# Softmax's end in two halves, an output sum in two parts, and phi's last steps moved, in a fused attention and FFN kernel on one core

## The chip, the core and the metric

The kernel runs on one core of one Trainium2 chip. Its time is the device time of one execution in microseconds (us). Five engines matter here, each with an instruction queue of its own that is worked off in order: TensorE (PE, with PEld for its weight loads), VectorE (DVE), ScalarE (ACT), SyncE (SP, which here only issues DMAs) and the DMA engines behind SP's queue. An instruction that waits holds up everything behind it in its queue.

## What is computed

```python
def _attn_ref(q, k, v, phi):                 # 8 batches, 8 heads, seq 576, head_dim 64; phi has 32 columns
    a = phi - np.max(phi, axis=2, keepdims=True)      # softmax of phi along the sequence
    a = np.exp(a); a = a / (np.sum(a, axis=2, keepdims=True) + 1e-09)
    k_m = np.einsum('bhsm,bhsd->bhmd', a, k)          # 32 memory rows a head
    v_m = np.einsum('bhsm,bhsd->bhmd', a, v)
    scores = (1/8) * np.matmul(q, k_m.transpose(0, 1, 3, 2))
    scores = scores - np.max(scores, axis=-1, keepdims=True)
    attn = np.exp(scores); attn = attn / (np.sum(attn, axis=-1, keepdims=True) + 1e-09)
    return np.matmul(attn, v_m)

def _moe_ref(x, w_in, w_out):                # x: 4608 x 512, d_ff 2048
    h = x @ w_in
    g = h * (1.0 / (1.0 + np.exp(-h)))
    return g @ w_out
```

## The kernel before

The kernel works through the eight batches one after the other. While the FFN of batch b runs, the attention of batch n = b + 1 is prepared beside it, and phi of batch m = b + 2 is begun. The FFN's first weight is folded with the attention's values (`p_mm`), so the FFN reads the attention's probabilities directly. All large operands are split in a high and a low part (`hi`, `lo`), and each product is made of three matmuls.

For batches 2 to 7 the FFN has 16 **slots**, eight for each half of the sequence (`t`). In slot s

- PE makes `h` (L807, 12 matmuls), then the matmuls of the slot's events, then, by `finish`, the 21 products L846 of the slot before (`st_step`);
- ACT applies Silu to `h` (L821 and L823; `gbuf` is one buffer), and makes high parts (L825, L835);
- DVE forms sums in `gbuf` (L826, L829, L830) and makes low parts (L836, L837). These five DVE instructions are called F(s) below.

The products are summed by a Strassen-like scheme in four PSUM banks (`sums`). After each half, `st_out` copies two banks on ACT (L877), adds on DVE (L882, seven adds) and stores two tiles of 128x512. The four banks are used again by the next half, so its products wait for the last add that reads them. After batches 1, 3, 5 and 7 a **left-over pass** handles the last 64 rows of two batches: `left_split` (L680, L682) splits `gleft` in four pieces, and L846 multiplies them into `lsum`.

The other work is put in slots by a table of events: `ev(b, slot, fn, ...)`. Events of one slot run in the order in which they were put there, after that slot's F(s). For slots (not for the left-over pass) every DVE instruction of an event is tied behind the slot's last split (`behind`); the framework's scheduler then sets the final order in each queue. Around the change these events stand:

- `s_max`, `s_sub`, `s_exp`, `s_sum`, `s_norm` (L424 to L442): the scores' softmax of batch n, slots 9 to 13, on the whole sequence `ALL`.
- `s_back` (slot 14): DVE transposes the probabilities (L454, two of 128x576), ACT writes the high part of the half `FIRST` (L459, in `s_high`), `s_low` the low part (L464). The other half, `SECOND`, gets its parts in slot 1 of the next batch.
- `p_mm` (L628): a fold into PSUM tile `bg`, of which there is one; ACT and DVE read it (L644, L646) before the next `p_mm` may write it. Slots 13 and 15, and slots 1 and 2 of the next batch.
- `phi_max`, `phi_fold`, `phi_sub`, for batch m: the maximum over the sequence. `phi_fold` turns it with a transpose (L284, L286), gathers four rows of 32 partitions side by side by four small copies (L292), reduces (L294), spreads the result by three small copies (L296), and turns it back (L301, L302); `phi_sub` subtracts it (L310, L313). Slots 11 and 15; for batch 2, slots 13 and 15.
- `win_load`: SP loads a quarter of the saved first weight (1 MB) in slots 10, 12 and 14 and in slot 0 of the next batch; each waits until PE is through with that place's last reader.

SP's queue is in order as well: loads, stores and anything else that it issues wait behind one another.

Of the kernel before, what the change touches and what calls it, by code (L numbers as in the profile page):

```python
# [10 lines left out]
F32 = mybir.dt.float32  # L11
# [14 lines left out]
NFC = DFF // P  # L26
CW = 256
JW = 512
NJ = DFF // JW
HALF = S // 2  # L30
MAIN = 512
LEFT = S - MAIN
NI = MAIN // P
# [15 lines left out]
def attn_ffn_kernel(  # L49
# [9 lines left out]
    nc = tc.nc  # L59
    const = ctx.enter_context(tc.tile_pool(name="const", bufs=1))  # L60
    sb = ctx.enter_context(tc.tile_pool(name="sb", bufs=2))
# [216 lines left out]
            for i, p in enumerate(ps_):  # L278
                at[b]["am", p] = pm[:, i * P : (i + 1) * P]

    def phi_fold(b, step):
        if step == 0:
            t = sb.tile([P, HM], F32, tag="am", name="mxt", bufs=1)
            nc.vector.transpose(t, at[b]["mx"].rearrange("p g f -> p (g f)"))  # L284
            qm = sb.tile([P, H], F32, tag="qm", name="qm", bufs=1)
            nc.vector.tensor_reduce(qm, t.rearrange("p (n m) -> p n m", m=M), op=ALU.max, axis=AX.X)  # L286
            at[b]["qm"] = qm
        elif step == 1:
            qm = at[b]["qm"]
            z = sb.tile([M, 4, H], F32, tag="qz", name="qz", bufs=1)  # L290
            for i in range(4):
                nc.vector.tensor_copy(z[:, i], qm[M * i : M * (i + 1)])  # L292
            fm = sb.tile([P, H], F32, tag="fm", name="fm", bufs=1)
            nc.vector.tensor_reduce(fm[:M], z.rearrange("p i n -> p n i"), op=ALU.max, axis=AX.X)  # L294
            for i in range(1, 4):
                nc.vector.tensor_copy(fm[M * i : M * (i + 1)], fm[:M])  # L296
            at[b]["fm"] = fm
        else:
            am = sb.tile([P, HM], F32, tag="am", name="am", bufs=1)
            wide = sb.tile([P, H, M], F32, tag="mx", name="wide", bufs=1)  # L300
            nc.vector.tensor_copy(wide, at[b]["fm"].unsqueeze(2).broadcast_to([P, H, M]))  # L301
            nc.vector.transpose(am, wide.rearrange("p n m -> p (n m)"))  # L302
            for p in range(2):
                at[b]["am", p] = am[:, p * P : (p + 1) * P]
# [139 lines left out]
    def set_parts(b):  # L444
        for k, x in enumerate(("ahi", "alo")):
            at[b][x] = aparts[:, k, b == 1].rearrange("p (g s) -> p g s", g=2)

    def s_back(b, u):
        tag = ("x", "y")[b - 1] if b < 3 else "q1"
        at[b]["aT"] = sb.tile([P, 2, S], F32, tag=tag, name=f"aT{b}", bufs=1)  # L450
        set_parts(b)
        aT, sc = at[b]["aT"], at[b]["sc"]
        for p in range(2):
            nc.vector.transpose(aT[:, p], sc[:, p])  # L454
        s_high(b, u)

    def s_high(b, u):
        c = slice(*u)
        nc.scalar.activation(at[b]["ahi"][:, :, c], at[b]["aT"][:, :, c], AF.Copy)  # L459

    def s_low(b, u):
        aT, ahi, alo = (at[b][k] for k in ("aT", "ahi", "alo"))
        c = slice(*u)
        nc.vector.tensor_tensor(alo[:, :, c], aT[:, :, c], ahi[:, :, c], op=ALU.subtract)  # L464

# [208 lines left out]
    def split(g32, steps=(0, 1), gs=None):  # L674
        if gs is None:
            n = next(turn) % 2
            gs = gparts[:, 0, n], gparts[:, 1, n]
        ghi, glo = gs
        if 0 in steps:
            nc.vector.tensor_copy(ghi, g32)  # L680
# [59 lines left out]
    Q = DMODEL // 2  # L740
# [114 lines left out]
    def st_step(b, t, j, part):  # L855
# [14 lines left out]
        if j == NP - 1:  # L870
            st_out(b, t)

    def st_out(b, t):
        o = sb.tile([P, 2, DMODEL], F32, tag="cva", name="oo", bufs=1)
        x = sb.tile([P, 2, Q], F32, tag="cva1", name="x", bufs=1)
        for i in range(2):
            nc.scalar.activation(o[:, i], sums[i], AF.Copy)  # L877
        (c11, c12), (c21, c22) = ((o[:, i, :Q], o[:, i, Q:]) for i in range(2))
        u2, u3 = x[:, 0], x[:, 1]

        def add(to, a, c, op=ALU.add):
            nc.vector.tensor_tensor(to, a, c, op=op)  # L882

        add(u2, sums[2][:, :Q], c11)
        add(u3, sums[2][:, Q:], u2)
        add(c11, c11, c12)
        add(c12, u2, c22)
        add(c12, c12, c21)
        add(c21, u3, sums[3][:, :Q], ALU.subtract)
        add(c22, u3, c22)  # L890
        for i in range(2):
            r = b * S + (2 * t + 1 - i) * P
            nc.sync.dma_start(out[r : r + P], o[:, i])
# [35 lines left out]
    def ev(b, slot, fn, *a):  # L929
        events.setdefault((b, slot), []).append((fn, a))  # L930

    def steady(b, n):


        early = b > 2
        if not early:
            ev(b, 1, phi_max, n)
            for i in range(3):
                ev(b, 2, phi_fold, n, i)
            ev(b, 3, phi_sub, n)  # L940
# [12 lines left out]
        ev(b, 13, s_norm, n, ALL)  # L953
        ev(b, 14, s_back, n, FIRST)
        ev(b, 14, s_low, n, FIRST)
        for k in range(3):
            ev(b, 10 + 2 * k, win_load, n, k)
        for k in range(2):
            ev(b, 13 + 2 * k, p_mm, n, k * JW, JW)
        m = n + 1  # L960
        if m < B:
            ev(b, ex + 3, load_kv, m, range(2))
            ev(b, ex + 3, load_phi, m)
            ev(b, ex + 5, load_q, m, 0)
            ev(b, 7 if early else 12, phi_max, m)
            for i in range(3):
                ev(b, 11 if early else 13, phi_fold, m, i)
            ev(b, 15, phi_sub, m)

    for b in range(B):  # L970
        n = b + 1
        if b == 0:
            for j in range(2, DFF // CW):
                ev(b, 2 * j - 1.5, p_mm, b, j * CW, CW)
        elif b == 1:
            ev(b, 0, win_save)
            for j in range(1, NJ):
                ev(b, 4 * j - 3, p_mm, b, j * JW, JW)
            for j in range(NP):
                ev(b, 1.5 * j + 2, w_forms, j, 0)  # L980
                ev(b, 1.5 * j + 2.5, w_forms, j, 1)
        else:
            ev(b, 0, win_load, b, 3)
            ev(b, 1, p_mm, b, 2 * JW, JW)
            if b > 2:
                ev(b, 1, s_high, b, SECOND)
                ev(b, 1, s_low, b, SECOND)
            ev(b, 2, p_mm, b, 3 * JW, JW)
            if n < B:
                steady(b, n)  # L990
            continue
# [176 lines left out]
    for b in range(B):  # L1168
# [3 lines left out]
        for s in range(NFC if b > 1 else 0):  # L1172
            t, j = divmod(s, NP)
            h = ffn1s(b, t, j)
            part = forms(b, t, j, h)
            for half_slot in range(2):
                for fn, a in events.pop((b, s + half_slot / 2), []):
                    traced = nc.cur_bb.bb.instructions
                    n = len(traced)
                    fn(*a)  # L1180
                    for i in list(nc.cur_bb.bb.instructions)[n:]:
                        if i.engine == DVE and fn is not s_all:
                            behind(i, last_split[-1])
            finish(range(NI))
            prev = ("st", b, t, j, part)
        for fc in range(NFC if b < 2 else 0):
# [23 lines left out]
        if b % 2:  # L1210
            for n in range(NLS):
                gs = left_split(b, n)
                finish((0, 1, 2, 3))
                prev = ("left", b, n, gs)
    finish((0,))
# [55 lines left out]
```

## Time and profile before

| what | value |
|---|---|
| runs | 709.49, 709.56, 711.04 us; median 709.56 us |
| profiled execution | 710.63 us; span from first to last instruction 708.8 us |
| mean granted TensorE clock | 0.994 |
| busy: PE, PEld, DVE, ACT | 681.1, 599.3, 521.9, 361.1 us |
| slots of batches 2 to 7, left-over passes | from about 200 us to the end |

A profile's line of groups reads: line, engine, operation, output<-inputs, shapes, count, then busy time, mean ns of one, and the idle time of the engine ahead of it with what ended it. In a timeline each row is start, duration, engine and instruction; the bracket is the engine's idle time just before and who ended it. Busy times of matmuls overlap: a matmul of 256 columns stands with 0.28 us, but the next one starts 0.12 us later, so that intervals between starts are what PE's pace is read from.

### The profile page before, as it was taken

To read this page: it belongs to the slowest core of one execution; us is meant where nothing else is said; L and a number is where in the kernel's file an instruction comes from. 1 tells how busy PE (TensorE), PEld (TensorE's weight loads), DVE (VectorE), ACT (ScalarE), POOL (GpSimd) and SP (SyncE) were. 2 spreads that over 40 slices of the span, in tenths; PEclk is the share of its full clock that TensorE was granted. 3 is DMA by queue.
4 is the path that set the end of the run, shared out by engine and by line. 5 is a ranking of instruction groups with operands and counts; after the bars stand their busy time and mean duration, and the time that the engine had idled before them with its cause. 6 is when DMAs were issued, how large, how long until landed. Compare 5 with 4: busy or idle time off the path is not lost.

```text
span 708.8 us, 14734 instructions
## 1 busy us (share of the span) xinstructions
PE 681.1 (96%) x5932; PEld 599.3 (85%) x5932; DVE 521.9 (74%) x1109; ACT 361.1 (51%) x664; POOL 0.7 (0%) x6
## 2 busy tenths in 40 slices
PE   8999999999999998899989999999998999999997
PEld 3578777888789898799978999789988899889996
DVE  4898799788847679748976489856885657775653
ACT  3879674534435454743625446464551635554440
POOL 0000000000000000000000000000000000000000
PEclk9999999999999999999999999999999999999999
DMA  9997965314441442243321433234430304310001
GB/s 344 337 349 253 324 253 214 107 43 157 164 137 60 159 149 104 79 154 123 122 90 49 168 121 123 88 96 143 149 120 31 109 2 137 123 40 1 31 1 45
DMA packets 32947, 93.89 MB, mean 132 GB/s; under 512 B 2928, under 2 KB 13296, under 8 KB 29296
## 3 DMA queue, kind: packets, MB, share of 16 engines
q1 hardware_dynamic: 31936, 90.19, 36.8%
q10 hardware_dynamic: 944, 2.77, 1.0%
q8 instruction: 47, 0.77, 0.4%
q14 instruction: 20, 0.16, 0.1%
HBM read 77.22 MB, written 15.73 MB: 131 GB/s over the span
## 4 chain that ended last, share of the span: by engine, by line
PE 61%; DVE 17%; issue 4%; ACT 4%; DVEq 0%; ACTq 0%
PE sum L846 23%; PE h L807 16%; PE acc L706 7%; PE lsum L846 5%; PE h L665 4%; PE bg L628 2%; DVE oo L882 2%; ACT aparts L835 2%; DVE pm L646 2%; DVE gbuf L826 2%; PE accleft L706 2%; PE bg L333 1%; DVE gbuf L829 1%; DVE gbuf L830 1%; DVE aT L454 1%
## 5 line engine op out<-in xcount | busy, mean ns | idle before, releaser
L807 PE MATMUL h<-aparts,pm 128*128 128x288 f32 x1152 | 169.0, 296 | 2.2 <-ACT gleft L823 2.2
L807 PEld LDWEIGHTS h<-aparts,pm 128*128 128x128 f32 x1152 | 157.1, 188 | 3.4 <-ACT gleft L823 2.5
L821 ACT ACTIVATE gbuf<-h 128x512 f32<-128x512 f32 x96 | 57.3, 597 | 140.7 <-PE h L807 140.4
L826 DVE TENSOR_TENSOR gbuf<-gbuf 128x256 f32<-128x256 f32 x96 | 40.4, 421 | 102.8 <-ACT gbuf L821 102.6
L846 PE MATMUL sum<-kept,aparts 128*128 128x256 f32 x576 | 100.8, 284 | 6.4 <-DVE oo L882 6.4
L846 PE MATMUL sum<-wo_hi,aparts 128*128 128x256 f32 x384 | 104.5, 294 | 0.7 <-ACT oo L877 0.7
L846 PE MATMUL sum<-wo_lo,aparts 128*128 128x256 f32 x384 | 100.0, 282 | 0.0
L835 ACT ACTIVATE aparts<-gbuf 128x512 fp32r<-128x512 f32 x86 | 54.4, 633 | 82.7 <-DVE gbuf L830 82.7
L846 PEld LDWEIGHTS sum<-wo_hi,aparts 128*128 128x128 f32 x384 | 72.7, 189 | 22.5 <-ACT gleft L823 10.9
L846 PEld LDWEIGHTS sum<-kept,aparts 128*128 128x128 f32 x576 | 82.5, 191 | 8.0 <-DVE oo L882 8.0
L706 PE MATMUL acc<-wo_hi,gparts 128*128 128x512 f32 x256 | 86.5, 397 | 0.2
L846 PEld LDWEIGHTS sum<-wo_lo,aparts 128*128 128x128 f32 x384 | 73.1, 190 | 0.0
L846 PE MATMUL sum<-wo_hi,gparts 128*128 128x256 f32 x384 | 72.7, 281 | 0.0
L837 DVE TENSOR_TENSOR gparts<-gbuf,aparts 128x512 fp32r<-128x512 f32 x86 | 59.4, 691 | 18.0 <-ACT aparts L835 18.0
L846 PE MATMUL sum<-kept,gparts 128*128 128x256 f32 x288 | 65.5, 282 | 0.0
L706 PEld LDWEIGHTS acc<-wo_hi,gparts 128*128 128x128 f32 x256 | 47.8, 188 | 14.5 <-DVE t L789 1.7
L846 PEld LDWEIGHTS sum<-wo_hi,gparts 128*128 128x128 f32 x384 | 59.4, 190 | 0.0
L665 PEld LDWEIGHTS h<-aparts,pm 128*128 128x128 f32 x372 | 51.8, 188 | 7.7 <-issue 2.3
L665 PE MATMUL h<-aparts,pm 128*128 128x288 f32 x372 | 56.3, 299 | 1.3 <-DVE aparts L464 1.0
L706 PE MATMUL acc<-wo_lo,gparts 128*128 128x512 f32 x128 | 50.5, 394 | 0.8 <-DVE wo_lo L182 0.7
L825 ACT ACTIVATE aparts<-gbuf 128x384 fp32r<-128x384 f32 x96 | 50.4, 525 | 0.0
L846 PEld LDWEIGHTS sum<-kept,gparts 128*128 128x128 f32 x288 | 47.9, 190 | 0.0
(200 smaller groups left out, 995.2 us busy)
## 6 DMA issues: line engine op xcount, KB each, us to landing
win<-win_saved SPq DMA_DIRECT2D x24, 1024.0 KB, 4.8
kv<-in_kv SPq DMA_DIRECT2D x28, 516.0 KB, 4.8
q<-in_q SPq DMA_DIRECT2D x16, 576.0 KB, 5.2
raw<-in_w_in SPq DMA_DIRECT2D x14, 512.0 KB, 7.4
out<-oo SPq DMA_DIRECT2D x27, 256.0 KB, 2.1
raw<-in_w_out SPq DMA_DIRECT2D x6, 1024.0 KB, 5.7
win_saved<-win SPq DMA_DIRECT2D x4, 1024.0 KB, 8.6
phi<-in_phi SPq DMA_DIRECT2D x7, 576.0 KB, 5.8
```

What stands on the lines that cost most here:

```text
L628: nc.tensor.matmul(bg[M * r : M * (r + 1), p, :w].rearrange("p (k f) -> p k f", f=P), kvT[D * p : D * (p + 1), 1, r], src[D * p : D * (p + ...
L646: nc.vector.tensor_tensor(lo[:, :, c], bg[:, :, :w], hi[:, :, c], op=ALU.subtract)
L665: nc.tensor.matmul(h[:, hf, :HALF], wt[:, p, fs], a[:, p, hf * HALF : (hf + 1) * HALF], start=n[hf] == 0, stop=n[hf] == 5, skip_group_chec ...
L706: nc.tensor.matmul(acc[key], gt[:, cs], wt[:, fc], start=fc == 0 and n == 0, stop=fc == NFC - 1 and n == 2)
L807: nc.tensor.matmul(h[:, i, :HALF], wt[:, p, f : f + P], a[:, p], start=n == 0, stop=n == 5)
L821: nc.scalar.activation(gbuf[:, :MAIN].rearrange("p (i f) -> p i f", i=2), h[:, :, :w], AF.Silu)
L825: nc.scalar.activation(hi[:, :3], g[:, 1:4], AF.Copy)
L826: nc.vector.tensor_tensor(g[:, 4:6], g[:, :1].broadcast_to([P, 2, P]), g[:, 1:3], op=ALU.subtract)
L835: nc.scalar.activation(hi[:, 3:], g[:, 4:], AF.Copy)
L837: last_split.append(nc.vector.tensor_tensor(lo[:, 3:], g[:, 4:], hi[:, 3:], op=ALU.subtract))
L846: nc.tensor.matmul(sums[bank][:, place * Q : (place + 1) * Q], gt[:, k], wt, start=bank not in begun, stop=True, skip_group_check=True,)
L882: nc.vector.tensor_tensor(to, a, c, op=op)
```

## The change

1. `s_norm` and `s_back` work on halves. `FIRST` is normalised in slot 13 and turned in slot 14; `SECOND` in slots 3 and 4 of the next batch (only for batches after 2). The turned half lies in the buffer `cva` (then shared with the output tile) and no more in `q1`.
2. `st_out` adds in another order: four adds and two stores of 128x256 come at once, and the three others with two stores (`rest`) are put first in the next slot's events.
3. `phi_sub` for batch m moves from slot 15 to the left-over pass (odd b) or to slot 1 of the next batch (even b).
4. In `steady`, the seven small copies of `phi_fold` for batch m become DMAs on SP's queue (`load`); for b > 2 its three steps are spread over slots 11, 12 and 13, for b = 2 over 13, 14 and 15.
5. The second `p_mm` moves from slot 15 to slot 14.
6. `left_split` makes the high part on ACT (from batch 3 on).

```diff
-    def phi_fold(b, step):
+    def phi_fold(b, step, move=nc.vector.tensor_copy):
...
-                nc.vector.tensor_copy(z[:, i], qm[M * i : M * (i + 1)])
+                move(z[:, i], qm[M * i : M * (i + 1)])
...
-                nc.vector.tensor_copy(fm[M * i : M * (i + 1)], fm[:M])
+                move(fm[M * i : M * (i + 1)], fm[:M])
...
     def s_back(b, u):
-        tag = ("x", "y")[b - 1] if b < 3 else "q1"
-        at[b]["aT"] = sb.tile([P, 2, S], F32, tag=tag, name=f"aT{b}", bufs=1)
-        set_parts(b)
-        aT, sc = at[b]["aT"], at[b]["sc"]
+        if "aT" not in at[b]:
+            at[b]["aT"] = {}
+            set_parts(b)
+        w = u[1] - u[0]
+        tag = "cva" if b > 2 else ("x", "y")[b - 1]
+        aT = at[b]["aT"][u] = sb.tile([P, 2, w], F32, tag=tag, name=f"aT{b}", bufs=1)
+        c = slice(*u)
         for p in range(2):
-            nc.vector.transpose(aT[:, p], sc[:, p])
-        s_high(b, u)
-
-    def s_high(b, u):
+            nc.vector.transpose(aT[:, p], at[b]["sc"][:, p, c])
+        nc.scalar.activation(at[b]["ahi"][:, :, c], aT, AF.Copy)
...
-        (c11, c12), (c21, c22) = ((o[:, i, :Q], o[:, i, Q:]) for i in range(2))
-        u2, u3 = x[:, 0], x[:, 1]
+        (c11, c21), (p3, p5) = ((o[:, i, :Q], o[:, i, Q:]) for i in range(2))
+        c12, c22 = x[:, 0], x[:, 1]
+        r = b * S + 2 * t * P
+        one, two = slice(r + P, r + 2 * P), slice(r, r + P)
...
-        add(u2, sums[2][:, :Q], c11)
-        add(u3, sums[2][:, Q:], u2)
-        add(c11, c11, c12)
-        add(c12, u2, c22)
-        add(c12, c12, c21)
-        add(c21, u3, sums[3][:, :Q], ALU.subtract)
-        add(c22, u3, c22)
-        for i in range(2):
-            r = b * S + (2 * t + 1 - i) * P
-            nc.sync.dma_start(out[r : r + P], o[:, i])
+        add(c12, sums[2][:, :Q], c11)
+        add(c22, sums[2][:, Q:], c12)
+        add(c11, c11, c21)
+        add(c21, c22, sums[3][:, :Q], ALU.subtract)
+        nc.sync.dma_start(out[one, :Q], c11)
+        nc.sync.dma_start(out[two, :Q], c21)
+
+        def rest():
+            add(c22, c22, p5)
+            add(c12, c12, p5)
+            add(c12, c12, p3)
+            nc.sync.dma_start(out[two, Q:], c22)
+            nc.sync.dma_start(out[one, Q:], c12)
+
+        late.append(rest)
...
-        return split(
-            gleft[:, n * NI : (n + 1) * NI].rearrange("p c f -> p (c f)"),
-            gs=None if b == 1 and n < 3 else (home[:, :MAIN], home[:, MAIN : 2 * MAIN]),
-        )
+        if b == 1:
+            return split(g, gs=gs if n == 3 else None)
+        nc.scalar.activation(gs[0], g, AF.Copy)
+        nc.vector.tensor_tensor(gs[1], g, gs[0], op=ALU.subtract)
+        return gs
...
-        ev(b, 13, s_norm, n, ALL)
+        ev(b, 13, s_norm, n, FIRST)
...
-            ev(b, 13 + 2 * k, p_mm, n, k * JW, JW)
+            ev(b, 13 + k, p_mm, n, k * JW, JW)
...
-                ev(b, 11 if early else 13, phi_fold, m, i)
-            ev(b, 15, phi_sub, m)
+                ev(b, 11 + i if early else 13 + i, phi_fold, m, i, load)
+            ev(*((b, NFC + 1) if b % 2 else (b + 1, 1)), phi_sub, m)
...
-                ev(b, 1, s_high, b, SECOND)
-                ev(b, 1, s_low, b, SECOND)
+                ev(b, 3, s_norm, b, SECOND)
+                ev(b, 4, s_back, b, SECOND)
+                ev(b, 4, s_low, b, SECOND)
...
+            todo = [(fn, ()) for fn in late] + events.pop((b, s), [])
+            late.clear()
...
                 gs = left_split(b, n)
+                for fn, a in [(fn, ()) for fn in late] + events.pop((b, NFC + n), []):
+                    fn(*a)
+                late.clear()
                 finish((0, 1, 2, 3))
```

What the scheduler makes of it is seen in the queues. In DVE's queue at the end of batch 3 (an odd batch), from the normalisation in slot 13 to the start of F(15), there stood before (L826 begins an F, L836 and L837 end it):

```order
L442 TENSOR_TENSOR sc_3407<-sc_3407,ssm 128x1152
L646 TENSOR_TENSOR pm<-bg,pm 128x1024
L826 TENSOR_TENSOR gbuf<-gbuf 128x256
L829 TENSOR_TENSOR gbuf<-gbuf 128x128
L830 TENSOR_TENSOR gbuf<-gbuf 128x128
L836 TENSOR_TENSOR gparts<-gbuf,aparts 128x384
L837 TENSOR_TENSOR gparts<-gbuf,aparts 128x512
L454 STREAM_TRANSPOSE aT_3805<-sc_3407 128x576 x2
L464 TENSOR_TENSOR aparts<-aT_3805,aparts 128x2x288
L826 TENSOR_TENSOR gbuf<-gbuf 128x256
```

In the changed kernel every line number after the first edits moves by about one (L825 is L826 of before, L457 is L454, L645 is L646). The same stretch, from L301 (which follows L442 and L645 of slot 13) to the start of F(15):

```order
L301 COPY wide<-fm 128x256
L825 TENSOR_TENSOR gbuf<-gbuf 128x256
L302 STREAM_TRANSPOSE am<-wide 128x256
L828 TENSOR_TENSOR gbuf<-gbuf 128x128
L310 TENSOR_TENSOR phi_3321<-phi_3321,am 128x512
L829 TENSOR_TENSOR gbuf<-gbuf 128x128
L835 TENSOR_TENSOR gparts<-gbuf,aparts 128x384
L313 TENSOR_TENSOR phi_3321<-phi_3321,am 64x128
L310 TENSOR_TENSOR phi_3321<-phi_3321,am 128x512
L836 TENSOR_TENSOR gparts<-gbuf,aparts 128x512
L457 STREAM_TRANSPOSE aT_3815<-sc_3415 128x288 x2
L313 TENSOR_TENSOR phi_3321<-phi_3321,am 64x128
```

After these come L463, then L645 of the `p_mm` that now stands in slot 14, then F(15). The events of the left-over pass are not tied behind a split, and the scheduler has taken `phi_sub` (L310, L313) of batch 3 out of the left-over pass and up into F(14), ahead of F(15); before, it stood behind F(15). Batch 5 reads alike.

In an even batch, `phi_sub` stays where it was put. DVE's queue in slot 1 of batch 5, after F(1): here it stands ahead of L645, which frees `bg` for the next `p_mm`.

```order
L885 TENSOR_TENSOR x<-x,oo 128x256 x2
L310 TENSOR_TENSOR phi_4364<-phi_4364,am 128x512
L885 TENSOR_TENSOR x<-x,oo 128x256
L313 TENSOR_TENSOR phi_4364<-phi_4364,am 64x128
L310 TENSOR_TENSOR phi_4364<-phi_4364,am 128x512
L313 TENSOR_TENSOR phi_4364<-phi_4364,am 64x128
L645 TENSOR_TENSOR pm<-bg,pm 128x1024
```

On SP's queue at the end of batch 3 the small copies (`qz`, `fm`) stand between the 1 MB loads `win_1` and `win_2` and behind `win_2`; before, there was none:

```order
L88 DMA win_1_3700<-win_saved_84 128x2048
L88 DMA qz<-qm 32x8 x4
L88 DMA win_2_3820<-win_saved_85 128x2048
L88 DMA fm<-fm 32x8 x3
L88 DMA win_3_4042<-win_saved_86 128x2048
```

What moved: each of the two rounds of small copies now waits on SP for DVE, and for its turn behind a load.

More of the change, by code (lines that the diff above doesn't have):

```diff
@@ L448, in s_back, with s_low @@
     def s_back(b, u):
-        tag = ("x", "y")[b - 1] if b < 3 else "q1"
-        at[b]["aT"] = sb.tile([P, 2, S], F32, tag=tag, name=f"aT{b}", bufs=1)
-        set_parts(b)
-        aT, sc = at[b]["aT"], at[b]["sc"]
+        if "aT" not in at[b]:
[5 more added lines that the diff above has]
+        c = slice(*u)
         for p in range(2):
-            nc.vector.transpose(aT[:, p], sc[:, p])
-        s_high(b, u)
-    def s_high(b, u):
+            nc.vector.transpose(aT[:, p], at[b]["sc"][:, p, c])
+        nc.scalar.activation(at[b]["ahi"][:, :, c], aT, AF.Copy)
+    def s_low(b, u):
+        ahi, alo = (at[b][k] for k in ("ahi", "alo"))
         c = slice(*u)
[L459 to L464, printed above, removed]
+        nc.vector.tensor_tensor(alo[:, :, c], at[b]["aT"][u], ahi[:, :, c], op=ALU.subtract)
     first = {}
@@ L871, in st_step @@
             st_out(b, t)
+    late = []
     def st_out(b, t):
@@ L897, in left_split @@
         home = (aparts[:, 0, 1], flat, flat[:, 2 * MAIN :], aparts[:, 1, 1])[n]
-        return split(
-            gleft[:, n * NI : (n + 1) * NI].rearrange("p c f -> p (c f)"),
-            gs=None if b == 1 and n < 3 else (home[:, :MAIN], home[:, MAIN : 2 * MAIN]),
-        )
+        g = gleft[:, n * NI : (n + 1) * NI].rearrange("p c f -> p (c f)")
+        gs = home[:, :MAIN], home[:, MAIN : 2 * MAIN]
+        if b == 1:
[3 more added lines that the diff above has]
+        return gs
     def left_st(b, n, gs):
@@ L1175, in attn_ffn_kernel @@
             part = forms(b, t, j, h)
[L1176 to L1183, printed above, removed]
+            todo = [(fn, ()) for fn in late] + events.pop((b, s), [])
+            late.clear()
+            for fn, a in todo:
+                traced = nc.cur_bb.bb.instructions
+                n = len(traced)
+                fn(*a)
+                for i in list(nc.cur_bb.bb.instructions)[n:]:
+                    if i.engine == DVE and fn is not s_all:
+                        behind(i, last_split[-1])
             finish(range(NI))
```

1 line of the change is left out of this document (added).

## The prediction

> **What bounds the kernel now.** The page comes first, with the busy times:
>
> ```profile
> PE 681.1 (96%) x5932; PEld 599.3 (85%) x5932; DVE 521.9 (74%) x1109; ACT 361.1 (51%) x664; POOL 0.7 (0%) x6
> ```
>
> PE is busy for 681.1 of 708.8 us. The change takes no matmul away, so it can win only from the 27.7 us in which PE idles, and from matmuls that run slower than they could. The waits say who holds PE (engine, line and who it waited for; total, times, longest):
>
> ```profile
> PE sum L846 <- DVE oo L882: 6.4, 8, 1.5
> PE lsum L846 <- DVE aparts L680: 4.1, 2, 2.1
> ```
>
> Two places: the products that wait for the last add of `st_out`, and the left-over pass that waits for DVE. The chain of work shows the first, in slot 9 of batch 3:
>
> ```profile
> 328.19 1.10 DVE oo L882 x3
> 329.33 1.57 PE sum L846 x11
> 330.90 1.60 PE h L807 x12
> 332.51 2.49 PE sum L846 x21
> ```
>
> A free slot is 1.60 + 2.49, about 4.1 us. PE's timeline shows this slot longer, and the end of batch 3:
>
> ```profile
> 325.71 1.76 PE L807 MATMUL h<-aparts,pm 128*128 128x288 f32 x12
> 330.74 1.77 PE L807 MATMUL h<-aparts,pm 128*128 128x288 f32 x12
> 343.06 1.76 PE L807 MATMUL h<-aparts,pm 128*128 128x288 f32 x12
> 352.46 1.76 PE L807 MATMUL h<-aparts,pm 128*128 128x288 f32 x12
> 362.76 0.48 PE L846 MATMUL lsum<-wo_hi,aparts 128*128 128x256 f32 x1 [2.05 <-DVE aparts L680]
> ```
>
> From 352.46, DVE decides until the pass starts. Its own rows:
>
> ```profile
> 349.23 1.35 DVE L442 TENSOR_TENSOR sc<-sc,ssm 128x1152 f32<-128x1152 f32 x1
> 350.50 1.22 DVE L646 TENSOR_TENSOR pm<-bg,pm 128x1024 fp32r<-128x1024 f32 x1
> 354.00 1.43 DVE L454 STREAM_TRANSPOSE aT<-sc 128x576 f32<-128x576 f32 x2
> 356.19 0.76 DVE L464 TENSOR_TENSOR aparts<-aT,aparts 128x576 fp32r<-128x576 f32 x1 [0.75 <-ACT aparts L459]
> 356.87 0.42 DVE L826 TENSOR_TENSOR gbuf<-gbuf 128x256 f32<-128x256 f32 x1
> 358.63 0.69 DVE L837 TENSOR_TENSOR gparts<-gbuf,aparts 128x512 fp32r<-128x512 f32 x1 [0.23 <-ACT aparts L835]
> 359.24 0.68 DVE L310 TENSOR_TENSOR phi<-phi,am 128x512 f32<-128x512 f32 x1
> 361.87 0.29 DVE L313 TENSOR_TENSOR phi<-phi,am 64x128 f32<-64x128 f32 x1
> 362.18 0.43 DVE L680 CAST aparts<-gleft 128x512 fp32r<-128x512 f32 x1
> ```
>
> DVE has hardly a gap from 349 to 363, and `phi_sub` and L646 stand between F(15) and the left-over split. Then the clock, by windows (length, busy PE, PEld, DVE, ACT, POOL with counts, granted clock, DMA share, GB/s), and three rows of the chain:
>
> ```profile
> 287.74:291.16 3.42, 1.96 (x15) 1.75 (x15) 3.19 (x10) 1.48 (x3) 0.00 (x0) 1.00 0.38 140
> 359.42:362.84 3.42, 1.37 (x12) 1.20 (x12) 3.38 (x7) 1.18 (x3) 0.00 (x0) 1.00 0.00 0
> 362.84:366.25 3.41, 3.26 (x14) 2.96 (x15) 3.41 (x9) 0.00 (x0) 0.00 (x0) 0.50 0.00 0
> 363.60 9.81 PE lsum L846 x70
> 373.41 1.58 PE h L807 x12
> 692.25 11.79 PE lsum L846 x96
> ```
>
> After a window with 1.37 us of matmuls the next one had half the clock; after one with 1.96 us there was no loss. At batch 7's rate, 0.121 us a matmul (11.79 for 96, less the 0.28 that the last one itself takes), 70 take 8.5 us and not 9.81: the slow clock costs 1.3.
>
> **Term A: the adds.** Slot 9 lasts 330.74 - 325.71 = 5.03, a free one 4.10: 0.93 lost. The last add that reads a bank is the seventh, at 329.29; in the new order it is the fourth, three adds of together 1.10 earlier, about 328.19. PE would be there at 329.33 - 0.93 = 328.40, so the wait goes. The three `rest` adds and two stores come behind F of the next slot, where DVE waits for Silu. Batch 2 loses 0.66 there, batches 3 to 7 0.93 each: 5 x 0.93 + 0.66 = 5.3 us. The row of waits bounds it at 6.4, from below at 4.7 if 0.1 stays in each.
>
> **Term B: the ends of batches 3 and 5.** I follow the queues with the durations of rows. All is 0.93 earlier by term A, so h of slot 13 starts at 342.11. What the new steps cost is read from these groups and rows:
>
> ```profile
> L292 DVE COPY qz<-qm 32x8 f32<-32x8 f32 x24 | 3.8, 160 | 0.4
> L302 DVE STREAM_TRANSPOSE am<-wide 128x256 f32<-128x256 f32 x6 | 2.6, 438 | 0.2
> 327.50 0.33 SPq L88 DMA_DIRECT2D win<-win_saved  x1
> 328.69 1.02 SPq L893 DMA_DIRECT2D out<-oo  x2
> win<-win_saved SPq DMA_DIRECT2D x1, 1024.0 KB, 5.8
> out<-oo SPq DMA_DIRECT2D x2, 256.0 KB, 5.2
> win<-win_saved SPq DMA_DIRECT2D x24, 1024.0 KB, 4.8
> out<-oo SPq DMA_DIRECT2D x27, 256.0 KB, 2.1
> ```
>
> - Taken from DVE: seven copies of 0.16, 1.1 us a fold. A normalisation of half the size is 1.35 / 2 plus a bit, 0.74 (a 128x576 operation, L464, takes 0.76); two transposes of 288 columns about 0.47 each, between 0.44 (256 columns, L302) and 0.72 (half of 1.43, for 576), for 1.43; L464 of half the size about 0.45. The other half's work goes to slots 3 and 4 of the next batch, where DVE idles for Silu each slot: nothing there.
> - Seven DMAs instead. Two stores issued at 328.69 behind a 1 MB load issued at 327.50 landed after 5.2 us, 0.6 behind the load (at 333.3); with nothing ahead 2.1. The first round is issued when the maxima are turned, from about 340.2, four in a row to 341.5, with nothing ahead: with 2.1 to 2.4 it lands by 343.9, and its reader L294 stands at 344.95. The second is issued from 345.2, behind the load issued at about 343.9; that lands at 343.9 + 4.8 = 348.7, the copies at 349.0 to 349.4. Their reader, L301, comes at 349.45. So I take no stall, with a margin near zero: this is the term that I know least. Ends of the range: no stall, or 2.1 behind the load's landing, 350.8, a stall of 1.35.
> - The second `p_mm` in slot 14 waits for L645 of the first (349.54), because there is one `bg`: PE loses 0.45.
> - `phi_sub` (0.68 + 0.29 twice, 1.9 us) now stands in F(14), ahead of F(15). From 349.45 come L301 and L302 (0.3 + 0.44), F(14) (359.24 - 356.87 = 2.4, waits for ACT included) and these 1.9, to 354.5. The two transposes (0.95), ACT's high part and L463 (0.35 + 0.45, half of the 0.75 and 0.76 of before), and L645 (1.22) bring F(15) to 357.4, *later* than 356.87 before. Its high part comes 358.63 - 356.87 = 1.76 behind that, at 359.1; PE needs it at 358.05, waits 1.07, and ends its products at 360.9.
> - The gain comes behind it. The split's high part is made on ACT beside the copies of L877 and needs no turn behind `phi_sub` on DVE: the left-over matmuls start at 361.15 instead of 362.76. PE idles less in the stretch before (0.45 and 1.07 in two windows, not 2.05 in one), so the clock stays, and 72 matmuls take 8.7 instead of 10.49. The next h starts at 361.15 + 8.7 = 369.85, before at 373.25 (373.41 by the chain, whose pieces leave out issue): 3.4, less the 0.93 of A: 2.45, twice 4.9 us.
>
> **Term C: the ends of batches 2, 4 and 6.** In batch 2 DVE decides from slot 14 to slot 1 of batch 3:
>
> ```profile
> 271.19 1.76 PE L807 MATMUL h<-aparts,pm 128*128 128x288 f32 x12
> 291.16 1.75 PE L807 MATMUL h<-aparts,pm 128*128 128x288 f32 x12
> 463.13 1.09 PE L628 MATMUL bg<-win,kvT 64*32 64x512 f32 x16 [0.69 <-DVE pm L646]
> 631.58 1.09 PE L628 MATMUL bg<-win,kvT 64*32 64x512 f32 x16 [0.43 <-DVE pm L646]
> ```
>
> From the first to the second row PE works through three slots and two `p_mm` of 1.1: 3 x 4.1 + 2.2 = 14.5 of 19.97, 5.5 lost. Halving and copies take 0.6 + 0.5 + 0.3 + 1.1 = 2.5 us off DVE there. Against it, `p_mm` in slot 14 waits 2.3 us for L645 in slot 13, and `phi_sub` ahead of L645 in slot 1 makes the next `p_mm` wait 1.9. Followed slot by slot, 1.0 is won beyond A. In batch 4 the wait of 0.69 before that `p_mm` grows to 1.95 by the same `phi_sub`, against gains at the batch's end: 0.1. Batch 6 has no phi: 0.3 of the 0.43. Sum 1.4. Ends: -1.3 (only the longer wait in batch 4 counts, 1.95 - 0.69) and 4 (all 2.5 of DVE's time in batch 2, 1.1 in batch 4, 0.4 in batch 6).
>
> **The sum.** 5.3 + 4.9 + 1.4 = 11.6 us of 710.63, the profiled execution: 699.0. It stands 1.07 above the median of the runs, so 709.56 - 11.6 = 698.0.
>
> **Rivals.**
> 1. The small copies pay a whole transfer behind the load. For it: 2.1 for a store alone. Against it: 0.6 behind the load at 328.69, so most of the 2.1 ran beside it. Price 1.35 in batches 3 and 5, 0.2 in 4: 698.0 + 2.9 = 700.9. [...]
> 2. The half clock stays in the left-over pass: 2 x 1.3, 700.6. For it: in my working PE still idles 0.45 + 1.07 = 1.52 before the pass, and both may fall in one window. Against it: 3.42 - 1.96 = 1.46 cost nothing, 2.05 did; 1.52 is nearer the harmless one. [...]
> 3. Only A comes: F(15) behind `phi_sub`, and the paired `p_mm`, give back what the ends win. 709.56 - 5.3 = 704.3. For it: F(15) starts later in my own working. Against it: what starts the left-over pass before is L680 at 362.18, 2.9 us after F(15) ended (358.63 + 0.69), and that part goes in any case.
> 4. DVE's relief goes through: the 0.45 and 1.07 in batches 3 and 5 vanish too, and C reaches its 4: 698.0 - 2 x 1.52 - 2.6 = 692.4. For it: DVE is 74% busy, so the work has room elsewhere. Against it: one `bg` for two folds in a row.
> 5. Slower: the four folds stall DVE, in whose queue F stands, and so PE. The longest median of the page's transfers is
>
> ```profile
> win_saved<-win SPq DMA_DIRECT2D x4, 1024.0 KB, 8.6
> ```
>
> To cancel 11.6 us each fold must stall by 2.9: second copies that land at 352.4, 7.2 us after their issue. From there on the kernel is slower; at 8.6, 1.4 more, it takes 709.56 + 4 x 1.4 = 715. Against it: nothing small took more than 5.2 here, and that behind a load.
>
> That `phi_sub` sits in the left-over pass is not so in odd batches (the order shows it in F(14)); were it so, F(15) would come 1.9 earlier. In even batches the change does what it says.
>
> **Chances.** Forecast 0.57 (694.7 to 701), rival 1 0.16, 2 0.07, 3 0.06, 4 0.04, 5 0.10. The range 694.0 to 704.5 holds the forecast and rivals 1 to 3, 0.86; its lower end leaves a part of rival 4's way open. A measurement of this kernel can't tell less than 0.3%, 2.1 us, from no change. Rival 5 splits in 0.04 within that and 0.06 slower; all else is faster, 0.90.
>
> **What will show it.** A: no wait for the adds of `st_out` in slot 9, free slots of 4.1. B: small copies landing within 4.2 us of issue and no idle time before L294 and L301; a left-over pass of 8.7 us at clock 1.00, started by ACT. C: waits of PE at `p_mm` for L645 near 2 us in batches 2 and 4. I am wrong if DVE waits on DMAs at L301, or if SP's loads come late because they wait behind the copies, and h or `p_mm` waits for `win`.

## The result, and the profile after

| kernel | us, all runs | median |
|---|---|---|
| before | 709.49, 709.56, 709.95, 711.04 | 709.75 |
| changed | 698.91, 701.35, 703.30, 703.95 | 702.33 |

The ratio is 0.9885, 95% interval 0.9844 to 0.9926: 7.4 us less at the medians, where 11.6 were forecast. The runs of the changed kernel lie 5 us apart, those of before 1.6. Beside each run stands the mean clock that it was granted: 698.91 with 0.999, 701.35 with 0.996, 703.30 with 0.994, 703.95 with 0.992. That order is the key to the result.

The profiled execution is the one of 701.35 us. Its page has these busy times, and its waits say who holds PE now:

```profile
PE 677.5 (97%) x5932; PEld 596.8 (85%) x5932; DVE 513.8 (73%) x1084; ACT 367.8 (53%) x676; POOL 0.7 (0%) x6
PE bg L627 <- DVE pm L645: 7.0, 7, 2.3
PE sum L845 <- ACT aparts L834: 1.8, 2, 0.9
DVE wide L301 <- DMA fm<-fm: 2.5, 3, 1.1
```

The waits for the adds of `st_out` and for the left-over split are gone. In their place PE waits 7.0 us for L645, which frees `bg`. (L301's wait for the DMAs is the sign by which the prediction called itself wrong; it is taken up below.) PE's timeline around slots 9, 13, 14 and 15 of batch 3 and the start of batch 4:

```profile
326.08 1.76 PE L806 MATMUL h<-aparts,pm 128*128 128x288 f32 x12
330.17 1.76 PE L806 MATMUL h<-aparts,pm 128*128 128x288 f32 x12
342.50 1.76 PE L806 MATMUL h<-aparts,pm 128*128 128x288 f32 x12
349.82 1.09 PE L627 MATMUL bg<-win,kvT 64*32 64x512 f32 x16 [0.27 <-DVE pm L645]
353.44 1.76 PE L806 MATMUL h<-aparts,pm 128*128 128x288 f32 x12
359.71 0.39 PE L845 MATMUL sum<-wo_hi,aparts 128*128 128x256 f32 x1 [0.88 <-ACT aparts L834]
370.59 1.75 PE L806 MATMUL h<-aparts,pm 128*128 128x288 f32 x12
```

Slot 9 takes 330.17 - 326.08 = 4.09. From slot 15 to the next batch it is 370.59 - 353.44 = 17.15 against 373.25 - 352.46 = 20.79. The chain of work for the pass, and DVE's rows for the fold and for F(15) of batch 3:

```profile
361.21 0.61 ACT oo L878
361.86 8.89 PE lsum L845 x72
350.54 0.29 DVE L301 COPY wide<-fm 128x256 f32<-128x256 f32 x1 [0.78 <-DMA fm<-fm]
357.93 0.41 DVE L825 TENSOR_TENSOR gbuf<-gbuf 128x256 f32<-128x256 f32 x1
```

ACT starts the pass, at full clock. No DMA stands on the chain at this end. The clock's loss stands elsewhere. In batch 2, slot 14, the second `p_mm` waits for L645 of slot 13. First its row on PE's timeline, then windows (columns as in the prediction), the one with the wait and the one behind it:

```profile
270.92 1.91 PE L627 MATMUL bg<-win,kvT 64*32 64x512 f32 x16 [2.28 <-DVE pm L645]
267.66:271.06 3.40, 1.12 (x16) 0.89 (x22) 3.17 (x6) 2.58 (x5) 0.00 (x0) 1.00 0.00 0
271.06:274.48 3.42, 3.42 (x24) 1.77 (x17) 3.15 (x9) 0.63 (x1) 0.00 (x0) 0.50 0.02 1
```

### The profile page after: what moved, and what is told of

Same layout as the page of the kernel before. It is cut to its first block, busy times and chain, and to the rows that moved or that the text cites. A ratio compares the mean times of both kernels' runs of the same rounds, so it can differ in the third digit from the quotient of the medians.

```text
span 699.5 us, 14791 instructions
## 1 busy us (share of the span) xinstructions
PE 677.5 (97%) x5932; PEld 596.8 (85%) x5932; DVE 513.8 (73%) x1084; ACT 367.8 (53%) x676; POOL 0.7 (0%) x6
## 3 DMA queue, kind: packets, MB, share of 16 engines
q10 hardware_dynamic: 944, 2.77, 1.0%
## 4 chain that ended last, share of the span: by engine, by line
PE 71%; DVE 8%; ACT 5%; issue 2%; DVEq 0%; ACTq 0%
PE sum L845 29%; PE h L806 18%; PE acc L705 7%; PE lsum L845 5%; PE h L664 4%; PE bg L627 3%; DVE pm L645 2%; PE accleft L705 2%; PE bg L333 1%; ACT aparts L834 1%; ACT gbuf L820 1%; DVE gbuf L825 1%; ACT L820 1%; ACT L432 1%; PE bg L380 1%
## 5 line engine op out<-in xcount | busy, mean ns | idle before, releaser
L825 DVE TENSOR_TENSOR gbuf<-gbuf 128x256 f32<-128x256 f32 x96 | 40.4, 421 | 94.3 <-ACT gbuf L820 93.8
L836 DVE TENSOR_TENSOR gparts<-gbuf,aparts 128x512 fp32r<-128x512 f32 x86 | 59.3, 690 | 18.0 <-ACT aparts L834 18.0
```

The costliest lines, as they stand in the source:

```text
L825: nc.vector.tensor_tensor(g[:, 4:6], g[:, :1].broadcast_to([P, 2, P]), g[:, 1:3], op=ALU.subtract)
L836: last_split.append(nc.vector.tensor_tensor(lo[:, 3:], g[:, 4:], hi[:, 3:], op=ALU.subtract))
```

## The experiments

Each was run with the kernel before on the same chip. There were three chips, on which the kernel before had medians of 711.06 (e0, e1, e3, e6), 710.59 (e2, e4, e5, e8) and 710.99 us (e7, e9, e10). Median and range are in us, with the mean clocks of the runs; the ratio is to the kernel before.

| kernel | median (range) | clocks | ratio, interval |
|---|---|---|---|
| e0_after | 701.13 (698.80 to 702.12) | 0.994 to 0.999 | 0.9857, 0.9838 to 0.9876 |
| e1_adds | 702.81 (701.70 to 704.48) | 0.993 to 0.999 | 0.9888, 0.9869 to 0.9907 |
| e2_fold_dve | 705.33 (704.10 to 705.45) | 0.993 to 0.997 | 0.9920, 0.9906 to 0.9935 |
| e3_pmm15 | 698.88 (698.21 to 699.18) | 0.994 to 0.995 | 0.9829, 0.9814 to 0.9843 |
| e4_phi_left | 699.35 (698.62 to 700.30) | 0.994 to 0.997 | 0.9843, 0.9824 to 0.9861 |
| e5_phi_even | 697.60 (696.17 to 697.76) | 0.996 to 0.999 | 0.9810, 0.9792 to 0.9828 |
| e6_all3 | 691.83 (691.64 to 692.10) | 0.998 to 0.999 | 0.9731, 0.9716 to 0.9745 |
| e7_all3_dve | 693.90 (693.68 to 694.00) | 0.998 to 1.000 | 0.9764, 0.9751 to 0.9778 |
| e8_split_dve | 703.11 (701.96 to 703.97) | 0.993 to 0.996 | 0.9892, 0.9875 to 0.9909 |
| e9_prod_first | 698.96 (697.04 to 700.60) | 0.994 to 1.000 | 0.9830, 0.9809 to 0.9850 |
| e10_best | 693.20 (692.79 to 693.87) | 0.998 to 1.000 | 0.9756, 0.9743 to 0.9769 |

**The changed kernel again (e0_after).**

> The changed kernel again, as it is. Theory (the clock's phase): an execution without a half-clock window takes 698.9, and each such window of 3.4 us adds 1.3 to 2.4 us and lowers the mean clock by 0.0024; so the times lie between 698.9 and about 704 and stand in the order of the mean clocks (0.999, 0.996, 0.994, 0.992). Rival (DMA landings decide): runs of the same mean clock differ by more than 1 us, or the order isn't that of the clocks.

698.80 with 0.999, 700.90 and 701.36 with 0.996, 702.12 with 0.994: the order of the clocks, and equal clocks within 0.5 us on this chip. The clock doesn't fix the time, though: 703.30 among the first four runs had 0.994 too, 1.2 us more than 702.12. This time the profile is of the execution without a half-clock window. The same place in batch 2, by PE's timeline and by windows on the grid that the clock's changes show (in the profile of before it falls to half at 362.84, 533.50 and 707.58, and 170.67 and 174.08 us are 50 and 51 windows of 3.41):

```profile
270.47 1.09 PE L627 MATMUL bg<-win,kvT 64*32 64x512 f32 x16 [2.27 <-DVE pm L645]
265.71:269.12 3.41, 2.49 (x20) 2.25 (x18) 3.14 (x9) 1.87 (x3) 0.00 (x0) 1.00 0.41 168
269.12:272.53 3.41, 2.06 (x24) 1.23 (x25) 3.24 (x8) 1.29 (x4) 0.00 (x0) 1.00 0.00 0
272.53:275.95 3.42, 3.42 (x30) 3.42 (x29) 2.53 (x6) 1.66 (x4) 0.00 (x0) 1.00 0.03 1
```

The wait is the same, 2.27 against 2.28. But here a window ends in its middle: the two windows hold 2.49 and 2.06 us of matmuls, not 1.12 in one, and the clock stays. Slot 14 took 7.65 us instead of 9.23. All other slots agree with the first profile within 0.3 us. So the one half-clock window there cost 1.58, and with the same wait none came here. Counted from the first instruction, the clock changes at 271.06 in the first profile and at 695.79 in this one, 124.4 windows apart and not a whole number; that it is the place of the 3.41 us windows under the program that decides is my reading of these two profiles, and no run shows it alone.

**The adds alone (e1_adds).** The kernel before, with the new `st_out`, `rest` and `late` and nothing else:

```diff
+        add(c21, c22, sums[3][:, :Q], ALU.subtract)
...
+        late.append(rest)
```

> The kernel before with the new order of st_out's adds and stores alone. Theory: the wait in slot 9 goes, six times, 5.3 us, the ends of the batches stay: 709.6 - 5.3 = 704.3 (703.8 to 704.8), slot 9 of 4.1 us. If the odd ends keep their gap of 2 us, two half-clock windows stay, mean clock 0.994. Rival: the first wait of a batch's end grows by what is won: 707 or more.

702.81, 1.5 us faster than was expected. Slot 9 is 4.09 in every batch from 3 on, 0.94 shorter, and 0.55 is won in batch 2: the 5.3 us are there. Between the profiles the spans differ by 8.1 us, and the rest has two parts. The clock is one: the gap ahead of batch 3's pass fell so that the window held 1.73 us of matmuls (the row is below), there was no half clock behind it, and this end took 1.0 less. The other wasn't expected, and isn't the clock: slots 0 to 2 of batches 3, 5 and 7 take 0.57, 0.74 and 0.51 less, 1.8 together. In slot 1 the three adds of `rest` now stand behind F, so that DVE comes sooner to F and then to L646, for which PE waits in slot 2: in batch 7 L646 starts 5.47 us after h of slot 1, before 6.17. The wait of 0.43 (the row at 631.58 in the prediction) there is gone:

```profile
624.40 1.09 PE L628 MATMUL bg<-win,kvT 64*32 64x512 f32 x16
```

The runs don't stand in the order of their clocks here: 704.48 had 0.994, 702.78 and 702.84 had 0.993, 701.70 had 0.999. The profile of 702.78 shows two reasons. One half-clock window lies in slot 0 of batch 3, where DVE is behind and PE waits for L646 again in slot 2; slots 0 to 2 took 17.04 with it, 17.61 before at full clock, so that no loss is seen. And the mean counts 2.4 us of half clock at the program's end, after the last matmul:

```profile
278.49:281.91 3.42, 3.42 (x16) 3.42 (x16) 3.12 (x7) 2.24 (x5) 0.00 (x0) 0.50 0.00 0
291.68 1.09 PE L628 MATMUL bg<-win,kvT 64*32 64x512 f32 x16 [0.57 <-DVE pm L646]
698.33:700.70 2.37, 0.00 (x0) 0.00 (x0) 0.00 (x0) 0.00 (x0) 0.00 (x0) 0.50 0.39 104
```

What makes the 2.8 us between e1's runs is not shown.

**The second p_mm back in slot 15 (e3_pmm15).**

```diff
-            ev(b, 13 + k, p_mm, n, k * JW, JW)
+            ev(b, 13 + 2 * k, p_mm, n, k * JW, JW)
```

> The changed kernel with the second p_mm back in slot 15. Theory: PE's wait for L645 in slot 14 goes (2.4 us in batch 2 with the half-clock window behind it, 0.35 in each other batch), F(15) of batches 3 and 5 starts 1.4 earlier; about 696 (694.5 to 697.5), mean clock 0.999 in most runs. Rival: the place of p_mm doesn't matter, the same wait comes back at F(15): 700 to 703 with the same spread.

698.88, less gain than expected by 2.9. Slot 14 of batch 2 takes 4.10 again, but every run has a clock of 0.994 to 0.995: in the profiled execution there are two half-clock windows in a row. PE's timeline and the windows show where, in slot 2 of batch 3:

```profile
290.68 1.96 PE L627 MATMUL bg<-win,kvT 64*32 64x512 f32 x16 [3.20 <-DVE pm L645]
286.43:289.84 3.41, 1.04 (x8) 0.81 (x7) 3.37 (x9) 1.56 (x4) 0.00 (x0) 1.00 0.22 77
289.84:293.25 3.41, 2.58 (x19) 0.92 (x20) 3.11 (x6) 0.51 (x1) 0.00 (x0) 0.50 0.00 0
```

PE comes earlier to the next `p_mm` that waits for L645, the one that `phi_sub` stands ahead of. That wait grows from 1.88 to 3.20, and the slow clock costs the rest: the slot went from 7.25 to 11.25. The gain was given back four slots later.

**phi_sub of odd batches really in the left-over pass (e4_phi_left).**

```diff
-        nc.vector.tensor_tensor(gs[1], g, gs[0], op=ALU.subtract)
+        last_split.append(nc.vector.tensor_tensor(gs[1], g, gs[0], op=ALU.subtract))
...
+                    for i in list(nc.cur_bb.bb.instructions)[k:]:
+                        if i.engine == DVE and fn is phi_sub:
+                            behind(i, last_split[-1])
```

> The changed kernel with phi_sub of odd batches tied behind the split of the left-over pass, nothing else. Theory: F(15) of batches 3 and 5 starts up to 1.9 earlier, PE's wait before the pass (1.8) shrinks by about 1.2 each: 698.9 - 2.4 = 696.5 (695.8 to 697.5) without a half-clock window, with batch 2's window 1.6 more. Rival: ACT's copies decide when the pass starts, F(15) doesn't: 698.5 or more without a window.

Slot 15 with the pass shrinks by 0.93 and 0.69 against e0_after, 1.6 for the expected 2.4; the rival is refuted in direction, not fully in size. No run had a clock above 0.997, so that the time without a half-clock window is not shown. DVE's F(15), and the two ends that matter on PE:

```profile
356.61 0.41 DVE L825 TENSOR_TENSOR gbuf<-gbuf 128x256 f32<-128x256 f32 x1
358.40 0.39 PE L845 MATMUL sum<-wo_hi,aparts 128*128 128x256 f32 x1 [0.17 <-ACT aparts L834]
360.54 0.39 PE L845 MATMUL lsum<-wo_hi,aparts 128*128 128x256 f32 x1
```

Counted from h of slot 15, F(15) starts 3.38 after it instead of 4.49 in the first profile, 1.1 earlier and not 1.9, and PE's wait for its high part falls from 0.88 to 0.17. `phi_sub` had stood in part in waits for ACT: between L301 and F(15) DVE waits 0.23, 0.75 and 0.15 for it here, 0.43 and 0.15 in the first profile. And with `phi_sub` gone the chain of work at this end goes through the second round of small copies, which it did in neither profile of the changed kernel; the piece of the chain, and DVE's row:

```profile
346.47 3.59 DMA fm<-fm
350.18 0.29 DVE L301 COPY wide<-fm 128x256 f32<-128x256 f32 x1 [0.64 <-DMA fm<-fm]
```

**phi_sub of even batches behind p_mm in slot 1 (e5_phi_even).**

```diff
-            ev(*((b, NFC + 1) if b % 2 else (b + 1, 1)), phi_sub, m)
+            if b % 2:
+                ev(b, NFC + 1, phi_sub, m)
...
             ev(b, 1, p_mm, b, 2 * JW, JW)
+            if b % 2 and n < B:
+                ev(b, 1, phi_sub, n)
```

> The changed kernel with phi_sub of even batches behind p_mm in slot 1 instead of ahead of it, nothing else. Theory: PE's wait of 1.95 for L645 in slot 2 goes in batches 3 and 5, some of it comes back at the exponential of phi in slot 3: 698.9 - 2.6 = 696.3 (695.3 to 697.5) without a half-clock window, with batch 2's window 1.6 more. Rival: DVE is full there and the wait only moves: 698.5 or more.

Slot 2 shrinks from 7.25 to 5.29 in batches 3 and 5, slot 3 grows by 0.6 each: 2.7 won. The run with a clock of 0.999 took 696.17, as expected without a half-clock window; the three others took 697.6 to 697.8 (0.996 to 0.997), and the profile of one of them has its half clock in batch 2.

**The split's high part on DVE again (e8_split_dve).**

```diff
-        nc.scalar.activation(gs[0], g, AF.Copy)
-        nc.vector.tensor_tensor(gs[1], g, gs[0], op=ALU.subtract)
-        return gs
+        return split(g, gs=gs)
```

> The changed kernel with left_split's high part on DVE again. The scheduler now draws the first two pairs of the split into F(15). Theory: F(15)'s low part comes 1.5 later in batches 3 and 5, and PE waits longer ahead of the pass: 698.9 + 3 = 701.9 (700 to 703) without a half-clock window, and with the longer gap such a window more often. Rival: the split's engine is indifferent, since ACT is busy with the copies at the same time: 698.9 (698.5 to 699.5).

703.11. Slot 15 with the pass grows by 1.99 and 1.09, 3.1 together, but not all of it at full clock. In batch 3 a half-clock window lies under the products ahead of the pass, which take 3.36 (360.29 to the pass at 363.65) instead of 2.15 in e0_after (357.52 to 359.67):

```profile
360.29 0.57 PE L845 MATMUL sum<-wo_hi,aparts 128*128 128x256 f32 x1 [1.58 <-ACT aparts L834]
363.65 0.33 PE L845 MATMUL lsum<-wo_hi,aparts 128*128 128x256 f32 x1
```

PE's wait for F(15)'s high part is 1.58 here, 0.88 in e0_after, since the split stands in F(15). So at full clock ACT's copy was worth about 1.9 and not 3; the other 1.2 came by the clock, as the expectation had said might happen more often.

**The small copies on DVE again (e2_fold_dve).**

```diff
-                ev(b, 11 + i if early else 13 + i, phi_fold, m, i, load)
+                ev(b, 11 + i if early else 13 + i, phi_fold, m, i)
```

> The changed kernel with the seven small copies of each fold on DVE again. Theory: DVE gets 1.1 us of copies back and loses its wait of 0.78 for the DMAs at L301, so without a half-clock window the time is 699.5 (698.8 to 700.7) instead of 698.9: the DMAs were worth next to nothing. Rival (the DMAs were a cause of the shortfall): 697 or less.

705.33: my theory fell, and so did the rival with its 697 or less. Against e0_after slot 14 of batches 3, 4 and 5 is longer by 1.59, 1.57 and 1.58. PE's timeline in batch 3, and DVE's rows ahead of it:

```profile
350.83 1.09 PE L627 MATMUL bg<-win,kvT 64*32 64x512 f32 x16 [1.86 <-DVE pm L645]
344.71 0.32 DVE L292 COPY qz<-qm 32x8 f32<-32x8 f32 x2
346.42 0.52 DVE L296 COPY fm<-fm 32x8 f32<-32x8 f32 x3
349.56 1.22 DVE L645 TENSOR_TENSOR pm<-bg,pm 128x1024 fp32r<-128x1024 f32 x1
```

The copies (L292, L296) stand ahead of L645 of slot 13, and with `p_mm` in slot 14 this L645 is what PE waits for: 1.86 instead of 0.27. I had counted only what DVE does behind it, where the DMAs cost a wait of 0.78 at L301. Slots 15 of batches 3 and 5 got 0.70 and 0.35 shorter. Net of the half clock, which the profile has in slot 14 of batch 2 and slot 2 of batch 5, the DMAs are worth 3 x 1.58 - 1.05 = 3.7 us.

**p_mm behind the products in slot 14 (e9_prod_first).** PE's order turned round, to fill the wait:

```diff
+            after = [e for e in todo if s == 14 and e[0] is p_mm]
+            run([e for e in todo if not (s == 14 and e[0] is p_mm)])
             finish(range(NI))
+            run(after)
```

`run` is the loop over the events as it was.

> The changed kernel with one order turned round on PE: in slot 14 the 21 products of slot 13 come ahead of p_mm, not behind it. DVE has the same work; only its L645 of slot 14 may come a little later. Theory: PE works through the wait for L645 of slot 13, so no window of 3.4 us at the end of batch 2 holds less than 2.2 us of matmuls, and no execution has a half-clock window there: all runs within 1 us of each other, mean clock 0.998 or 0.999. Of the 2.4 us of wait in batch 2 about 1.2 comes back at F(15); 0.36 is won in batches 3, 4 and 5: 698.9 - 2.6 = 696.3 (695.3 to 697.3). Rival (the spread has another cause than the gap in batch 2, DMA landings for one): runs still spread over 2 us or more, and the slowest reach 698 or more.

Slot 14 of batch 2 falls to 5.21, without a wait. But the runs still spread over 3.6 us, from 697.04 with a clock of 1.000 to 700.60 with 0.994: the rival's numbers. Its cause, though, isn't the rival's. The windows show the half clock at the waits of slot 2 in batches 3 and 5:

```profile
287.83:291.24 3.41, 1.07 (x17) 0.24 (x17) 3.19 (x8) 0.80 (x3) 0.00 (x0) 1.00 0.11 38
291.24:294.65 3.41, 3.41 (x19) 3.41 (x17) 2.61 (x3) 3.26 (x3) 0.00 (x0) 0.50 0.00 0
455.08:458.49 3.41, 1.38 (x19) 0.54 (x20) 3.19 (x7) 1.34 (x4) 0.00 (x0) 1.00 0.11 38
```

I took away one gap and had not looked at the next.

**All gaps taken away (e6_all3, e10_best).** e6_all3 joins the edits of e3, e4 and e5; e10_best those of e4, e5 and e9.

> The changed kernel with three places changed: the second p_mm back in slot 15, phi_sub of odd batches tied behind the split of the left-over pass, phi_sub of even batches behind p_mm in slot 1. Theory: beside the p_mm waits the 1.9 us at p_mm in slot 2 of batches 3 and 5 go, and about 1.2 us before each left-over pass of batches 3 and 5: 692 (690.5 to 694), hardly a half-clock window. Rival: the waits come back elsewhere, since DVE has the same work: 696 or more.

> The same turned order in slot 14, with phi_sub of odd batches tied behind the split of the left-over pass and phi_sub of even batches behind p_mm in slot 1. Theory: the terms add, 696.3 - 1.6 - 2.7 = 692.0 (690.8 to 693.0), without half-clock windows. Rival: DVE is now the bound at the batches' ends and the terms don't add: 693.5 or more.

691.83 lies near the middle of its range; 693.20 is 0.2 above its range and 0.3 below its rival. The clocks are 0.998 to 1.000, the spreads 0.5 and 1.1 us. In neither profile does any window of the grid after 200 us hold less than 2.2 us of matmuls, until the program ends. e6_all3 is the fastest version: 0.9731 of the kernel before, and about 9.3 us less than e0_after on its chip.

**The best version with the copies on DVE (e7_all3_dve).**

> The version with p_mm in slot 15 and both phi_subs moved (691.8), with the small copies back on DVE. Theory: the copies cost 1.6 us a batch in the changed kernel because L645 of slot 13, which p_mm in slot 14 waits for, stands behind them; with p_mm in slot 15 nothing waits there, and DVE's 1.1 us is hidden: 692.3 (691.6 to 693.2). Rival: DVE is the bound at the batches' ends in any case, 1.1 us in each of four batches: 695 or more.

693.90, 2.1 us slower than e6_all3 and 0.7 above the expected range; the rival's 695 isn't reached either. With no `p_mm` in slot 14 the copies cost half of what they cost in e2, mostly 0.63 in slot 15 of batches 3 and 5 (F(15) later).

**The half-clock windows side by side.** In the rows shown, a window at half clock stood behind full-clock windows of 3.41 us with 1.04 (e3), 1.07 and 1.38 (e9), 1.12 (the first profile) and 1.37 us of matmuls (before). Behind windows with 1.96 (before), 2.06 and 2.49 us (e0_after) the clock stayed full. On PE's timelines in e3, e8 and e9 the matmuls of 256 columns start 0.21 us apart at half clock, 0.12 at full. Two windows hold 1.73 each. Behind the first, in e8, the matmuls start 0.21 apart; behind the second, in e1, 0.12:

```profile
356.92:360.33 3.41, 1.73 (x13) 1.32 (x12) 3.41 (x9) 1.40 (x4) 0.00 (x0) 1.00 0.64 269
357.00:360.41 3.41, 1.73 (x15) 1.53 (x13) 3.37 (x7) 1.62 (x3) 0.00 (x0) 1.00 0.00 0
```

What decides between these two is not shown. In e3 PE stayed slow for a second window (starts 0.21 apart from 293.37 to about 296.5) after one that held 2.58 us of matmuls at half clock; that is one case.

## Why the prediction was right or wrong

The direction and the range (694.0 to 704.5) held; the forecast of 698.0 was too low by 4.3 us. Against the execution without a half-clock window the working can be taken term by term (starts of h, e0_after against before; the spans are 697.0 and 708.8):

| term | forecast | measured |
|---|---|---|
| A, slot 9, six times | -5.3 | -0.57 - 5 x 0.94 = -5.3 |
| B, ends of 3 and 5 | -4.9 | -2.25 - 2.77 = -5.0 |
| C, ends of 2, 4 and 6 | -1.4 | -0.99 - 0.21 - 0.27 = -1.5 |
| sum | -11.6 | -11.8 |

- **Term A** held, alone as well (e1_adds). But the adds do more than slot 9: at the starts of batches 3, 5 and 7 they win another 1.8 us, which the prediction did not follow there.
- **Term B** held in size. Inside it, the copies' own times (KB each, median us from issue to landing) were

```profile
qz<-qm SPq DMA_DIRECT2D x16, 1.0 KB, 1.7
fm<-fm SPq DMA_DIRECT2D x12, 1.0 KB, 4.0
```

  The second round, behind a load, kept L301 waiting 2.5 us in three folds (0.78 in batch 3), between no stall in the forecast and 1.35 in rival 1. By the trace the last copy landed 1.1, 1.8 and 0.9 us behind the load in batches 3, 4 and 5, where rival 1 had 2.1. So the prediction's own sign, DVE waiting at L301, came, and its reading of no stall was wrong; the price did not come, since the chain of work at these ends has no DMA in it. Counted from h of slot 13, F(15) started 15.43 after it (15.3 in the working), the pass 19.36 (19.04), and the pass took 8.73 instead of 8.7. What I did not see is how much the copies' leaving was worth through `p_mm` in slot 14; the sum had it right because the queue was followed, the reason I gave for the copies (hidden, 1.1 off DVE) was too small.
- **Term C** is the step that failed, in two ways. The first is the clock. I forecast the wait of `p_mm` in slot 14 of batch 2 (2.3 forecast, 2.28 measured), and costed it as a wait alone. It empties a window to 1.12 us, and the next one runs at half the clock: 1.58 in the profiled execution. So C, forecast at -1.4, came to +0.1 there. Rival 2 had the half clock in the wrong place: I asked for the left-over pass, where no half clock came in either profile, and not for batch 2, where I had just put a gap of 2.3 us. The second is where the gain comes from. At full clock C's number is met, but partly by luck: the working took it from DVE's relief by the halving and the copies, while the adds alone win 0.57, 0.74 and 0.51 in the same places (e1_adds). Against e1 the rest of the change wins 0.4 after batch 2 and loses 0.5 after batch 4, where `phi_sub` stands ahead of L645 in slot 1, and 0.2 after batch 6, where `p_mm` waits in slot 14.
- **The median** mixes executions with none to several such windows. The eight runs of the changed kernel are two of 698.8 to 698.9 (clock 0.999), three of 700.9 to 701.4 (0.996) and three of 702.1 to 704.0 (0.992 to 0.994). The forecast of 698.0 is that of the first group. Where the windows of the third group lie no profile shows; by e9 the waits of 1.88 in slot 2 of batches 3 and 5 are the likeliest places (e0_after's windows there held 1.83), but that is argued, not shown.
- Rivals 3 to 5 did not come. No fold stalled DVE at L301 by more than 1.1 us in the first profile, 1.3 in e0_after.

## What to carry to other kernels

Cost a wait of the busiest engine by what follows it on the clock too, not by its length alone: here a wait of 2.28 us left 1.12 us of matmuls in a window of 3.41 and cost 3.9 with the half clock behind it, and one of 2.27, which left 2.49 and 2.06, cost 2.3. The sign of it was a spread of 5 us that followed the granted clock (698.91 with 0.999 to 703.95 with 0.992). A half-clock window that lay where DVE was the bound, in e1, cost nothing that can be seen (slots 0 to 2 of batch 3 took 17.04, and 17.61 before at full clock). Two folds in a row through one PSUM tile turn everything on DVE ahead of the first fold's reader into PE's time, so look at what stands ahead of the freeing instruction, not only at what stands behind it. After one gap is closed, look at the next place where the same engine waits before counting the gain: in e3 and e9 the next `p_mm` took most of it back.

## What the runs showed of the hardware

- Windows at half clock stood behind full-clock windows of 3.41 us with 1.04 to 1.38 us of matmuls (before, the first profile, e3, e9); behind windows with 1.96 to 2.49 (before, e0_after) the clock stayed full. The matmuls of 256 columns started 0.21 us apart in half-clock windows (e3, e8, e9), 0.12 at full clock; behind two windows with 1.73 they started 0.21 apart in e8 and 0.12 in e1. Counted from the first instruction, the clock fell at 362.84 in the profile of before and at 271.06 in the first of the changed kernel, 26.9 windows apart and not a whole number.
- A half-clock window cost 1.3 us in the left-over pass of the kernel before (9.81 instead of 8.5, an estimate from batch 7's 11.79 for 96 matmuls), 1.58 in slot 14 of batch 2, and nothing that can be seen in slot 0 of batch 3 in e1 (17.04 for slots 0 to 2, before 17.61).
- The 16 DMAs of 1 KB of the first round (`qz`), issued 4.4 us or more behind a load of 1 MB, took 1.6 to 2.2 us from issue to landing in the first profile, 1.7 in the median. Those of the second (`fm`) in batches 3, 4 and 5, issued 1.2 to 2.6 us behind such a load, took 3.3 to 5.1, and landed 0.5 to 1.8 us after it (5.0 is the load's own median).
